# k^T v of six batches moved from the steady stage into the first batch's mixing

## The chip, the cores and the metric

The kernel runs on one core of a Trainium2 chip. The metric is device time in microseconds of one execution. TensorE (PE), VectorE (DVE), ScalarE (ACT) and GpSimd (POOL) compute; SyncE (SP) issues most of the transfers. Each engine works through its own list of instructions in order and waits for the others by semaphores.

## The reference

There are eight batches of 576 tokens, eight heads of 64. All of it is float32.

```python
kv  = einsum('bhsd,bhse->bhde', k, v)          # per head: k^T v, 64 x 64, over 576 tokens
out = einsum('bhsd,bhde->bhse', q, kv)
x   = out / sqrt(mean(out*out, -1) + 1e-6) * g_norm
theta = x @ w_theta                            # 512 x 512
y   = w_tok_r @ (x*cos(theta)) + w_tok_i @ (x*sin(theta))   # over tokens
u   = x + y;  x2 = u + relu(u @ w_ch)
h   = relu(x2^T @ w_tok1) @ w_tok2;  u2 = x2 + h^T
result = u2 + relu(u2 @ w_ch1) @ w_ch2         # 512 -> 1536 -> 512
```

## The kernel before

Most products are made of three float16 matmuls (a value is split into a high and a low half; high by high, high by low, low by high). Only k^T v (line 304), q times k^T v (line 324) and the transposes of batch 0 are float32 matmuls.

A batch goes through units, which are generators: each call of `go` first moves all pending units on by one step and then starts a new one. The units are `kv` (K, two parts per batch), `attend` (a or n, one per row tile r0 to r4), `rotate` (r: theta, sine and cosine, the operands zh and zl), `mix` (M, eight units of 27 matmuls: two column chunks by four output tiles), `channel` (C), `token1` (H) and `token2` (T). Strings and dictionaries in the loop over batches (lines 822 to 870) say which units of the next batches stand beside which unit of the current one. The order of instructions on each engine follows from there: a list scheduler takes the program's order as priority, lets ready instructions of lower priority run ahead, and gives out the eight PSUM banks (line 51) and the buffers of the tile pools as they come free. `urgent` and `placed` raise some instructions or tie them to others.

The row tiles of k and v have 128, 128, 128, 96 and 96 tokens (`ROWS`). `load_kv` (line 266) brings one row tile of k and of v by two transfers from SyncE. Batch 0's last two pairs have buffers in the pool `kp`; everything else goes through three buffers per tensor in the pool `fp`. `load_heads` issues the first three pairs of a batch and its q; the last two pairs are issued by `kv`, after the step that follows the part that frees a buffer. `kv` (line 295) multiplies a row tile of k with one of v for each head and sums over the row tiles in one PSUM bank; after the second part, ScalarE copies half the heads and VectorE the other half into the one operand `kvbd`, which is block-diagonal (two heads in 128 x 128) and was set to zero once on GpSimd (line 123). `attend` multiplies q by it.

Before the loop over batches stand batch 0's k^T v, attention and rotation, the decoding and splitting of the mixing weights, and batch 1's k^T v. The mixing units of batch 0 stand beside the attention of batch 1 and the decoding of w_ch. Batch 2's k^T v stands among the token units of batch 0, which run while batch 1 mixes; that of each later batch stands beside the channel and token units (K00 and K10 in `STEADY`, line 823). The pools `kp` and `stg` end after batch 0's mixing (line 837), and the pools for the later weights take their place. The last rotated tile of batch 0 (`rotate_last`) goes through a transposing transfer from zt into zh (line 457); the last third of the last operand of every mixing unit comes from it.

After the batches come eight pairs of chunks of the last two layers, which are bound by TensorE alone and not touched by the change.

Of the kernel before, what the change touches and what calls it, by code (L numbers as in the profile page):

```python
# [11 lines left out]
F32 = mybir.dt.float32  # L12
I32 = mybir.dt.int32
AF = mybir.ActivationFunctionType
# [5 lines left out]
P = 128  # L20
# [8 lines left out]
def attn_mixer_kernel(  # L29
# [4 lines left out]
    nc = tc.nc  # L34
    B, S, DM = k.shape
    D = g_norm.shape[0]
    H = DM // D
    KD = DM // P
    NR = S // P
# [7 lines left out]
    HP = H // 2  # L47
# [7 lines left out]
    const = const_ctx.enter_context(tc.tile_pool(name="const", bufs=1, side="left"))  # L55
    zp = mix_ctx.enter_context(tc.tile_pool(name="zp", bufs=2, side="left"))
    mp = mix_ctx.enter_context(tc.tile_pool(name="mp", bufs=1, side="left"))
    fp = front_ctx.enter_context(tc.tile_pool(name="fp", bufs=1, side="right"))
    kp = start_ctx.enter_context(tc.tile_pool(name="kp", bufs=2, side="right"))
# [59 lines left out]
    nc.gpsimd.memset(eps, 1e-6)  # L119
    hpi = const.tile([P, 1], F32, name="hpi")  # L120
    nc.gpsimd.memset(hpi, HALF_PI)
    kvbd = const.tile([P, HP, P], F32, name="kvbd")
    nc.gpsimd.memset(kvbd, 0.0)

    def pair(shape, name, pool=const):
        return pool.tile(shape, F16, name=name + "h", bufs=1), pool.tile(shape, F16, name=name + "l", bufs=1)
# [137 lines left out]
    KV = ((0, 1), (2, 3, 4))  # L264

    def load_kv(o, r):
        b, n = o.b, ROWS[r + 1] - ROWS[r]

        pool, bufs = (kp, 2) if b == 0 and r > 2 else (fp, 3)
        for t, src in (("k", k), ("v", v)):  # L270
            dst = pool.tile([P, DM], F32, tag=t, name=f"{t}{b}{r}", bufs=bufs)[:n]
            nc.sync.dma_start(dst, src[b, ROWS[r]:ROWS[r + 1], :])
            o.kv.append(dst)

    def load_heads(b):
        o = Batch()
        o.b, o.zh = b, None
        o.kv = []
        for r in range(3 if b else NR + 1):
            load_kv(o, r)  # L280
        o.q = fp.tile([P, HP, SM + P], F32, tag="q", name=f"q{b}", bufs=1)
        qs = qT[b].rearrange("h p s -> p h s")
        if b == 0:
            nc.sync.dma_start(o.q[:, :, :P], qs[:, :, :P])
        else:
            load_q(o, 0)
        return o
# [7 lines left out]
    def kv(o, part):  # L295

        if part == 0:
            o.kp = bank(f"kvp{o.b}")[:, :HP * D].rearrange("p (h e) -> p h e", h=HP)
        for r in KV[part]:
            kt, vt = o.kv[2 * r:2 * r + 2]  # L300
            for hp in range(HP):
                for i in range(2):
                    cs = slice((2 * hp + i) * D, (2 * hp + i + 1) * D)
                    nc.tensor.matmul(
                        o.kp[i * D:(i + 1) * D, hp, :], kt[:, cs], vt[:, cs],
                        start=r == 0 and hp == 0, stop=r == NR and hp == HP - 1,
                    )
        if part:
            nc.scalar.activation(kvbd[:D, :, :D], o.kp[:D], AF.Copy)
            nc.vector.tensor_copy(kvbd[D:, :, D:], o.kp[D:])  # L310
        yield
        for r in KV[part]:
            if len(o.kv) < 2 * (NR + 1):
                load_kv(o, r + 3)

    def attend(o, r):

        b = o.b
        if r == 0:
            o.R = mp.tile([P, KD, S], F32, tag="R", name=f"R{b}", bufs=2)  # L320
            o.x, o.xt = {}, {}
        po = bank(f"po{b}{r}")
        for hp in range(HP):
            nc.tensor.matmul(po[:, hp * P:(hp + 1) * P], o.q[:, hp, r * P:(r + 1) * P], kvbd[:, hp, :], start=True, stop=True)  # L324
        po3 = po.rearrange("p (h d) -> p h d", d=D)
        ss = fp.tile([P, H], F32, tag="ss", name=f"ss{b}{r}", bufs=3)
        ri = fp.tile([P, H], F32, tag="ri", name=f"ri{b}{r}", bufs=3)
        xs = fp.tile([P, 2, DM], F16, tag="xs", name=f"xs{b}{r}", bufs=2) if b else None
        x = o.x[r] = fp.tile([P, DM], F32, tag="x", name=f"x{b}{r}", bufs=NR + 1)
        xt = o.xt[r] = fp.tile([P, 2, KD, P], F16, tag="xt", name=f"xt{b}{r}", bufs=NR + 1)  # L330

        x3 = x.rearrange("p (h d) -> p h d", d=D)
        place = beside(o)
        yield
        place(nc.scalar.activation(x3, po3, AF.Square, scale=D**-0.5))
        yield
        place(nc.vector.tensor_reduce(ss, x3, axis=AX.X, op=ALU.add))
        nc.gpsimd.tensor_tensor(ss, ss, eps, ALU.add)
        nc.gpsimd.tensor_tensor(ri, ss, mhalf, ALU.pow)  # L339
        yield  # L340
        yield
        place(nc.vector.tensor_tensor(x3, po3, ri.unsqueeze(2).to_broadcast([P, H, D]), ALU.mult))
        n = SR if r == NR else P
        R, by = o.R[:, :, r * P:r * P + n], SW if r == NR else gs
        if b == 0:

            yield
            px = bank(f"px{r}").rearrange("p (k t) -> p k t", k=KD)
            for kk in range(KD):
                nc.tensor.transpose(px[:, kk, :], x[:, kk * P:(kk + 1) * P], ident)  # L350
            yield
            split(xt[:, 0], xt[:, 1], px, 1.0)
            nc.scalar.activation(R, px[:, :, :n], AF.Copy, scale=by)
            return
        if b > 1:
            yield
        place(nc.scalar.activation(xs[:, 0, :], x, AF.Copy))
        yield
        place(nc.vector.tensor_tensor(xs[:, 1, :], x, xs[:, 0, :], ALU.subtract))
        place(nc.sync.dma_start_transpose(xt.rearrange("p a k t -> p (a k) t"), xs.rearrange("p a d -> p (a d)")))  # L360
        for _ in range(3 if b > 1 else 2):
            yield
        place(nc.scalar.activation(R, xt[:, 0, :, :n], AF.Copy, scale=by))
        yield
        place(nc.vector.scalar_tensor_tensor(R, xt[:, 1, :, :n], by, R, ALU.mult, ALU.add))
# [374 lines left out]
    def go(unit, lead=False):  # L740
        advance()
        next(unit)
        (leading if lead else pending).append(unit)
# [16 lines left out]
    def spare(n=1):  # L760
        for _ in range(min(n, len(extra))):
            go(extra.pop(0))

    def front(unit, o, r):
        if o is not None:
            go(unit(o, r))

    tk, cp, first = [], [], iter(())
    for j in range(KD):
        if j == KD - 1:  # L770
            o = load_heads(0)
# [15 lines left out]
    nxt = load_heads(1)  # L787
# [6 lines left out]
    MIX, CHANNEL, TOKEN2 = ([f"{k}{c}{i}" for c in range(2) for i in range(KD)] for k in "MCT")  # L794
    TOKEN1 = [f"H{c}{i}" for c in range(2) for i in range(KJ)]
    UNITS = {"M": mix, "C": channel, "H": token1, "T": token2}

    def run(units, o, nxt, after, also):

        for u in units:  # L800
            kind, c, i = u[0], int(u[1]), int(u[2])
            if kind == "K":
                front(kv, after, c)
            else:
                go(UNITS[kind](o, c, i), True)
            for what in also.get(u, "").split():
                if what == "w":
                    spare()
                elif what == "l":
                    if o.b + 2 < B:  # L810
                        loaded.append(load_heads(o.b + 2))
                elif what[0] == "a":
                    front(attend, nxt, int(what[1]))
                elif what[0] == "n":
                    front(attend, after, int(what[1]))
                elif what[0] == "r":
                    front(rotate, nxt, int(what[1]))
                elif what == "f":
                    next(first, None)

    loaded = []
    TOKENS1 = ["K00", "H00", "H01", "K10", "H10", "H11"]
    STEADY = MIX[:6] + CHANNEL[:2] + MIX[6:] + CHANNEL[2:4] + ["K00"] + CHANNEL[4:] + TOKENS1[1:] + TOKEN2
    BESIDE = {
        "M00": "a2", "M01": "a3", "M02": "a4 l w", "M03": "r0", "M11": "r1", "M12": "r2",
        "C03": "r4", "C10": "w", "H01": "r3 w", "H11": "n0", "T01": "n1 w", "T12": "w",
# [1 line left out]
    for b in range(B):  # L828
        loaded.clear()
        if b == 0:  # L830
            run(MIX, o, nxt, None, {
                "M00": "a0 w", "M01": "a1 w", "M02": "a2 w", "M03": "a3 w", "M10": "a4 r0 w", "M11": "r1 l w", "M12": "r2 w", "M13": "w",
            })
            after = loaded[0]
            spare(len(extra))
# [5 lines left out]
            src, _ = words(w_tok1)  # L841
# [10 lines left out]
            before = o  # L852
        elif b == 1:
            run(MIX[:4], o, nxt, None, {})
            run(["K00"] + TOKEN1 + ["K10"] + TOKEN2, before, None, nxt, {"T00": "n0", "T02": "n1", "T10": "n2 w", "T12": "n3"})
            run(MIX[4:6] + CHANNEL[:1], o, nxt, None, {"M10": "a4 l"})
            after = loaded[0]
            run(STEADY[STEADY.index("C01"):], o, nxt, after, {
                "C01": "r0", "M12": "r1", "M13": "r2", "C03": "r4", "C10": "w", "H01": "r3 w", "H11": "n0", "T01": "n1 w", "T12": "w",
            })  # L860
        elif b + 2 < B:
            at = STEADY.index("M02") + 1
            run(STEADY[:at], o, nxt, None, BESIDE)
            after = loaded[0]
            run(STEADY[at:], o, nxt, after, BESIDE)
        elif b + 2 == B:
# [6 lines left out]
            before, after = o, None  # L873
# [17 lines left out]
        o, nxt = nxt, after  # L891
# [52 lines left out]
```

## Time and profile before

| | |
|---|---|
| three runs | 1104.88, 1108.42, 1108.13 us (median 1108.13) |
| the profiled execution | 1103.0 us, span 1101.2 us |
| mean granted TensorE clock | 0.994 |
| busy: PE, DVE, ACT, POOL | 1066.4, 812.7, 565.7, 186.7 us |
| transfers | 126.31 MB, mean 115 GB/s |

Times in the profile are counted from the start of the span. A busy TensorE counts overlapping matmuls once; a matmul's own duration is longer than the distance from its start to the next start. The granted clock is a mean over a stretch, as a share of full speed. In the timeline, the bracket behind a row is the idle time ahead of it and what ended it.

### The profile page before, as it was taken

The page shows a single profiled execution, that of the slowest core. Times are in us where ns is not written, and L with a number is a line of the kernel's source. Part 1 is how long each engine was busy: PE and PEld are TensorE (multiplying, and loading weights), DVE is VectorE, ACT ScalarE, POOL GpSimd, SP SyncE. Part 2 cuts the span into 40 slices and gives each one's busy share as a digit, 9 for nine tenths or more (in the row PEclk, how much of TensorE's full clock was granted, in tenths as well). Part 3 has the DMA queues.
Part 4 walks back from the last instruction along what each step waited for, and adds up shares of the span by engine and source line. Part 5 has one row for each costly group of instructions (what it writes and reads, how often), then busy time and mean ns, then how long its engine had stood idle before and what let it go on. Part 6 is the DMA issues. An engine that isn't in the chain of part 4 may idle for free.

```text
span 1101.2 us, 21603 instructions
## 1 busy us (share of the span) xinstructions
PE 1066.4 (97%) x8884; PEld 813.7 (74%) x8884; DVE 812.7 (74%) x1475; ACT 565.7 (51%) x966; POOL 186.7 (17%) x252
## 2 busy tenths in 40 slices
PE   4779999999999999999999999999999999999998
PEld 4466776767777678776877777777777777777776
DVE  4989868887988869877654685758586775758484
ACT  3857536556465654646431645446363645446360
POOL 2250032442814518243001000000000000000000
PEclk9989999999999999999999999999999999999999
DMA  9725675867748668472456402020201102020101
GB/s 311 263 69 144 139 193 130 227 156 186 230 107 222 172 165 242 96 175 69 102 205 202 162 23 65 11 76 2 85 3 39 50 22 66 12 76 1 44 1 44
DMA packets 146626, 126.31 MB, mean 115 GB/s; under 512 B 93216, under 2 KB 123040, under 8 KB 146528
## 3 DMA queue, kind: packets, MB, share of 16 engines
q1 hardware_dynamic: 141152, 104.49, 35.1%
q0 software_dynamic: 5376, 20.45, 5.1%
q8 instruction: 69, 1.13, 0.4%
q14 instruction: 29, 0.24, 0.1%
HBM read 74.25 MB, written 29.88 MB: 95 GB/s over the span
## 4 chain that ended last, share of the span: by engine, by line
PE 86%; DVE 7%; DMA 3%; ACT 1%; issue 1%; SPq 1%; POOL 0%; ACTq 0%; DVEq 0%
PE py L104 5%; PE py L105 5%; PE py L103 5%; PE na L103 4%; PE na L105 4%; PE pa L105 4%; PE pa L104 4%; PE pa L103 4%; PE na L104 4%; PE po L324 3%; PE pr L103 2%; PE pr L104 2%; PE pr L105 2%; PE pt L104 2%; PE nc L105 2%; PE nc L103 2%
## 5 line engine op out<-in xcount | busy, mean ns | idle before, releaser
L103 PE MATMUL py<-wmh,zh 128*128 128x256 f16 (+1 forms) x576 | 165.5, 288 | 3.9 <-DMA zh<-zt 2.4
L104 PE MATMUL py<-wml,zh 128*128 128x256 f16 (+1 forms) x576 | 165.4, 288 | 0.0
L105 PE MATMUL py<-wmh,zl 128*128 128x320 f16 (+1 forms) x512 | 146.4, 287 | 0.0
L105 PE MATMUL na<-gh,wbl 128*128 128x288 f16 x384 | 109.3, 286 | 0.0
L104 PE MATMUL pa<-o,wah 128*128 128x288 f16 x384 | 109.2, 286 | 0.0
L104 PE MATMUL na<-gl,wbh 128*128 128x288 f16 x384 | 109.1, 286 | 0.0
L103 PE MATMUL pa<-o,wah 128*128 128x288 f16 x384 | 108.4, 286 | 0.0
L105 PE MATMUL pa<-o,wal 128*128 128x288 f16 x384 | 107.8, 286 | 0.0
L103 PE MATMUL na<-gh,wbh 128*128 128x288 f16 x384 | 106.0, 286 | 0.2
L625 DVE TENSOR_TENSOR gl<-sum,gh 128x1152 f16<-128x1152 f32 x48 | 65.0, 1354 | 21.9 <-ACT gh L624 21.9
L104 PEld LDWEIGHTS <-wbh 128*128 128x128 f16 x672 | 65.7, 98 | 17.7 <-issue 1.0
L104 PEld LDWEIGHTS <-wah 128*128 128x128 f16 x672 | 65.8, 98 | 16.6
L103 PEld LDWEIGHTS <-wah 128*128 128x128 f16 x672 | 65.8, 98 | 16.6
L103 PEld LDWEIGHTS <-wbh 128*128 128x128 f16 x672 | 65.7, 98 | 16.6
L105 PEld LDWEIGHTS <-wal 128*128 128x128 f16 x672 | 65.8, 98 | 16.6
L105 PEld LDWEIGHTS <-wbl 128*128 128x128 f16 x672 | 65.7, 98 | 16.6
L105 PE MATMUL pr<-uh,wcl 128*128 128x256 f16 (+1 forms) x256 | 73.1, 286 | 0.0
L104 PE MATMUL pr<-ul,wch 128*128 128x256 f16 (+1 forms) x256 | 73.1, 286 | 0.0
L103 PE MATMUL pr<-uh,wch 128*128 128x256 f16 (+1 forms) x256 | 73.0, 286 | 0.0
L103 PEld LDWEIGHTS <-zh 128*128 128x128 f16 x576 | 56.7, 98 | 19.8 <-DMA zh<-zt 2.6
L339 POOL TENSOR_TENSOR ri<-ss,mhalf 128x8 f32<-128x8 f32 x40 | 68.8, 1720 | 2.5
L624 ACT ACTIVATE gh<-sum 128x1152 f16<-128x1152 f32 x48 | 55.5, 1156 | 25.6 <-DVE sum L672 25.6
(297 smaller groups left out, 2855.1 us busy)
## 6 DMA issues: line engine op xcount, KB each, us to landing
c<-u2d SPq DMA_DIRECT2D x32, 288.0 KB, 4.3
out<-c SPq DMA_DIRECT2D x64, 144.0 KB, 1.8
q<-in_q SPq DMA_DIRECT2D x7, 1152.0 KB, 6.5
k<-in_k SPq DMA_DIRECT2D x24, 256.0 KB, 5.6
v<-in_v SPq DMA_DIRECT2D x24, 256.0 KB, 5.7
wa_r<-in_w_ch SPq DMA_DIRECT2D x24, 256.0 KB, 4.1
wb_r<-in_w_ch SPq DMA_DIRECT2D x24, 256.0 KB, 4.4
wad<-wa POOLq DMA_DIRECT2D x24, 224.0 KB, 4.0
```

What stands on the lines that cost most here:

```text
L103: nc.tensor.matmul(acc, ah, bh, start=first and i == 0, stop=False, **more)
L104: nc.tensor.matmul(acc, ah, bl, start=False, stop=False, **more)
L105: nc.tensor.matmul(acc, al, bh, start=False, stop=last and i == n - 1, **more)
L324: nc.tensor.matmul(po[:, hp * P:(hp + 1) * P], o.q[:, hp, r * P:(r + 1) * P], kvbd[:, hp, :], start=True, stop=True)
L339: nc.gpsimd.tensor_tensor(ri, ss, mhalf, ALU.pow)
L624: nc.scalar.activation(h.hi[:, 3:], h.s, AF.Copy)
L625: nc.vector.tensor_tensor(h.lo[:, 3:], h.s, h.hi[:, 3:], ALU.subtract)
```

## The change

`kvbd` becomes a list of eight operands, one per batch, each set to zero at the start: those of batches 0 and 1 in `kp`, the others in `fp`, where the buffers of k and v were. k and v of all batches go through a ring of five buffers per tensor in `kp`. Batches 0 and 1 load all five pairs in `load_heads`. Each part of `kv` of batch 1 to 6 then issues the loads of the same row tiles of the next batch, which take the buffers that its matmuls free. The twelve parts of batches 2 to 7 stand in a list, `products`, and a new mark "k" in the dictionary of batch 0's mixing starts the next of them: two beside each of M00 to M03, M10 and M11. The units K00 and K10 leave the token units and `STEADY`. In `kv` the loads stand ahead of the yield.

```diff
-    kvbd = const.tile([P, HP, P], F32, name="kvbd")
-    nc.gpsimd.memset(kvbd, 0.0)
+    kvbd = [(fp if b > 1 else kp).tile([P, HP, P], F32, name=f"kvbd{b}", bufs=1) for b in range(B)]
+    for t in kvbd:
+        nc.gpsimd.memset(t, 0.0)
...
     def load_kv(o, r):
         b, n = o.b, ROWS[r + 1] - ROWS[r]
-
-        pool, bufs = (kp, 2) if b == 0 and r > 2 else (fp, 3)
         for t, src in (("k", k), ("v", v)):
-            dst = pool.tile([P, DM], F32, tag=t, name=f"{t}{b}{r}", bufs=bufs)[:n]
+            dst = kp.tile([P, DM], F32, tag=t, name=f"{t}{b}{r}", bufs=NR + 1)[:n]
...
+    batches = [Batch() for _ in range(B)]
+    for b, o in enumerate(batches):
+        o.b, o.zh, o.kv = b, None, []
+
     def load_heads(b):
-        o = Batch()
-        o.b, o.zh = b, None
-        o.kv = []
-        for r in range(3 if b else NR + 1):
-            load_kv(o, r)
+        o = batches[b]
+        if b < 2:
+            for r in range(NR + 1):
+                load_kv(o, r)
...
         if part:
-            nc.scalar.activation(kvbd[:D, :, :D], o.kp[:D], AF.Copy)
-            nc.vector.tensor_copy(kvbd[D:, :, D:], o.kp[D:])
-        yield
-        for r in KV[part]:
-            if len(o.kv) < 2 * (NR + 1):
-                load_kv(o, r + 3)
+            nc.scalar.activation(kvbd[o.b][:D, :, :D], o.kp[:D], AF.Copy)
+            nc.vector.tensor_copy(kvbd[o.b][D:, :, D:], o.kp[D:])
+        if 0 < o.b < B - 1:
+            for r in KV[part]:
+                load_kv(batches[o.b + 1], r)
+        yield
...
-            if kind == "K":
-                front(kv, after, c)
-            else:
-                go(UNITS[kind](o, c, i), True)
+            go(UNITS[kind](o, c, i), True)
...
+                elif what == "k":
+                    go(kv(*products.pop(0)))
...
-    TOKENS1 = ["K00", "H00", "H01", "K10", "H10", "H11"]
-    STEADY = MIX[:6] + CHANNEL[:2] + MIX[6:] + CHANNEL[2:4] + ["K00"] + CHANNEL[4:] + TOKENS1[1:] + TOKEN2
+    products = [(batches[b], part) for b in range(2, B) for part in range(2)]
+    STEADY = MIX[:6] + CHANNEL[:2] + MIX[6:] + CHANNEL[2:] + TOKEN1 + TOKEN2
...
-                "M00": "a0 w", "M01": "a1 w", "M02": "a2 w", "M03": "a3 w", "M10": "a4 r0 w", "M11": "r1 l w", "M12": "r2 w", "M13": "w",
+                "M00": "a0 k k w", "M01": "a1 k k w", "M02": "a2 k k w", "M03": "a3 k k w", "M10": "a4 k k r0 w",
+                "M11": "r1 l k k w", "M12": "r2 w", "M13": "w",
...
-            run(["K00"] + TOKEN1 + ["K10"] + TOKEN2, before, None, nxt, {"T00": "n0", "T02": "n1", "T10": "n2 w", "T12": "n3"})
+            run(TOKEN1 + TOKEN2, before, None, nxt, {"T00": "n0", "T02": "n1", "T10": "n2 w", "T12": "n3"})
```

## Rows read from the trace of the kernel before

**Rows 1.** The page: TensorE's share of the span, and its granted clock in 40 slices.

```profile
PE 1066.4 (97%) x8884; PEld 813.7 (74%) x8884; DVE 812.7 (74%) x1475; ACT 565.7 (51%) x966; POOL 186.7 (17%) x252
...
PE   4779999999999999999999999999999999999998
...
PEclk9989999999999999999999999999999999999999
```

**Rows 2.** Waits of TensorE, whole span: for whom, us in total, times, longest.

```profile
PE kvp L304 <- DMA v<-in_v: 14.9, 5, 10.4
...
PE py L103 <- DMA zh<-zt: 2.4, 1, 2.4
PE po L324 <- DVE x L342: 1.9, 1, 1.9
```

**Rows 3.** Stretches: busy time of each engine, granted clock, DMA share and GB/s.

```profile
18.00:36.00 18.00, 12.69 (x77) 10.00 (x73) 14.56 (x25) 10.98 (x19) 8.20 (x8) 1.00 1.04 393
47.00:57.00 10.00, 6.92 (x138) 5.79 (x133) 9.94 (x15) 7.53 (x13) 0.00 (x0) 0.81 0.77 249
57.00:67.00 10.00, 6.88 (x47) 5.75 (x46) 10.00 (x16) 9.44 (x16) 5.29 (x4) 0.84 0.26 96
67.00:77.00 10.00, 9.74 (x72) 8.41 (x73) 9.28 (x16) 4.08 (x9) 7.68 (x5) 0.83 0.00 0
77.00:87.00 10.00, 7.62 (x51) 5.48 (x50) 4.80 (x9) 3.41 (x8) 1.04 (x1) 0.85 0.59 119
87.00:97.00 10.00, 10.00 (x60) 5.83 (x59) 10.00 (x21) 6.78 (x14) 2.06 (x2) 0.98 0.88 250
140.00:480.00 340.00, 337.93 (x2963) 246.25 (x2962) 276.90 (x500) 189.22 (x342) 136.74 (x190) 1.00 0.69 179
```

**Rows 4.** Instructions on the tile kvp: count, duration ns (min/median/max), first and last start.

```profile
L304 PE MATMUL kvp<-v,k x640: 220/222/369, 10.4 to 476.5; 128*64 128x64 f32 x96, 96*64 96x64 f32 x64
...
L310 DVE COPY kvbd<-kvp x8: 427/428/428, 19.1 to 477.6; 64x256 f32<-64x256 f32 x8
```

**Rows 5.** Timeline of TensorE, 183 to 198 us: start, duration, what.

```profile
183.48 1.15 PE L304 MATMUL kvp<-v,k 128*64 128x64 f32 x32
184.56 0.31 PE L103 MATMUL pr<-uh,wch 128*128 128x320 f16 x1
...
196.37 1.62 PE L304 MATMUL kvp<-v,k 128*64 128x64 f32 x48
198.01 0.39 PE L535 MATMUL ph<-xt,w1h 128*128 128x512 f16 x1
```

**Rows 6.** Timeline of TensorE, 83 to 99 us: mixing units.

```profile
83.64 0.27 PE L105 MATMUL py<-wmh,zh 128*128 128x256 f16 x1
...
85.94 0.47 PE L105 MATMUL py<-wmh,zh 128*128 128x320 f16 x1
...
95.94 0.30 PE L105 MATMUL py<-wmh,zl 128*128 128x320 f16 x1
...
99.20 0.30 PE L105 MATMUL py<-wmh,zh 128*128 128x320 f16 x1
```

**Rows 7.** Timeline of VectorE at 79 us.

```profile
79.29 0.68 DVE L452 TENSOR_TENSOR zt<-cs,zt 128x512 f16<-128x512 f32 x1
```

**Rows 8.** Timeline of TensorE, 51 to 54 us: batch 1's product.

```profile
51.83 0.69 PE L304 MATMUL kvp<-v,k 96*64 96x64 f32 x16 [1.44 <-DMA v<-in_v]
53.19 1.06 PE L304 MATMUL kvp<-v,k 96*64 96x64 f32 x16 [0.68 <-DMA v<-in_v]
```

**Rows 9.** Timeline of GpSimd, 1 to 24 us.

```profile
1.33 0.52 POOL L123 MEMSET kvbd<- 128x512 f32 x1
...
23.16 0.58 POOL L338 TENSOR_TENSOR ss<-ss,eps 128x8 f32<-128x8 f32 x1 [18.81 <-DVE ss L337]
```

**Rows 10.** Timeline of SyncE's queue, 54 to 82 us.

```profile
54.66 0.44 SPq L272 DMA_DIRECT2D v<-in_v  x1
80.00 1.37 SPq L457 DMA_TRANSPOSE zh<-zt  x1
```

More of the change, by code (lines that the diff above doesn't have):

```diff
@@ L323, in attend @@
         for hp in range(HP):
-            nc.tensor.matmul(po[:, hp * P:(hp + 1) * P], o.q[:, hp, r * P:(r + 1) * P], kvbd[:, hp, :], start=True, stop=True)
+            nc.tensor.matmul(po[:, hp * P:(hp + 1) * P], o.q[:, hp, r * P:(r + 1) * P], kvbd[b][:, hp, :], start=True, stop=True)
         po3 = po.rearrange("p (h d) -> p h d", d=D)
```

## The prediction

> **What bounds the kernel now.** I read the page first. TensorE is busy 97% of the span, and in the 40 slices it is at 9 from the fourth on; its granted clock dips only at the start [rows 1]. So from about 90 us every microsecond of TensorE work is a microsecond of time, and nothing is lost ahead of it except near the start. The waits of TensorE name what is lost: 14.9 us for v (10.4 of it the first load, which the change leaves), then one late transpose of zt, one late x, one late zh [rows 2]. The stretches show where [rows 3] (the columns are the length, the busy time of PE, PEld, DVE, ACT and POOL, the granted clock, the DMA share and GB/s). Between 47 and 87 us TensorE is busy 6.92 + 6.88 + 9.74 + 7.62 = 31.2 of 40 us, so 8.8 us are idle, and its clock is 0.81 to 0.85 of full, which by two levels (1.2 and 2.4 GHz) means 0.19 + 0.16 + 0.17 + 0.15 of each ten us at half, doubled: 13.4 us at the lower level. Of these some 12 are busy, and half of that, 6 us, is work that the full clock would have done besides. In the same stretch VectorE is full (9.94 and 10.00 of 10) until about 77: it decodes and splits the mixing weights and rotates batch 0, and the last tile of batch 0 is what the mixing units wait for. From 140 to 480 TensorE is busy 337.9 of 340 at full clock. So there are 8.8 + 6 = 14.8 us of free room for TensorE between 47 and 87, and next to none after it.
>
> **The change, part by part.**
>
> *The products leave the steady stage.* One batch's k^T v is 80 matmul records (640 for eight batches [rows 4]). In the steady stage a block of 32 takes 183.48 to 184.56 and a block of 48 takes 196.37 to 198.01 until the next matmul starts [rows 5]: 1.08 + 1.64 = 2.72 us. Six batches: 16.3 us less there, on the path, since TensorE is full. Their twelve evacuations (0.43 us on VectorE each [rows 4]) leave too, from engines that have slack there (VectorE 276.9 of 340).
>
> *The same 16.3 us enter batch 0's mixing.* The work is conserved, so the gain is what part of the 14.8 us of room it fills, less what it delays. Four terms:
>
> (a) How much can be done before the mixing units get their last operand, at about 83.4 us. k and v of a batch are 2 x 576 x 512 x 4 bytes = 2.36 MB. At the 393 GB/s that the transfers reached between 18 and 36 [rows 3] that is 6.0 us, at the 249 GB/s of 47 to 57 it is 9.5. The ring holds one batch, so batch 2 starts to load as batch 1's rows are consumed, at about 47, and can be done at 55 to 58; by 83.4 five batches fit at the upper rate, three at the lower. The transfers stood at 96 and 0 GB/s from 57 to 77, so the engines of the DMA are free; I take four: 4 x 2.72 = 10.9 us.
>
> (b) What they push out. PSUM has eight banks. Before the late operand, five mixing units stand in five banks, each with 24 of its 27 matmuls done; their last ones run 83.64 to 85.94 [rows 6]. A product waiting for its evacuation holds a bank. A unit of 256 columns costs, by M12's 3.26 us between its first and ninth low product [rows 6] scaled by 256/320, 2.6 us. I take one and a half units that no longer run ahead: 3.9 us; bounds 0 and 5.2.
>
> (c) What they do to VectorE. Four copies ahead of the last tile's subtraction at 79.29 [rows 7], behind which the transpose and the mixing units stand: 4 x 0.43 = 1.7 us. An evacuation queued behind a product that lacks its load would also hold ScalarE and VectorE; bound: in batch 1 TensorE waited 1.44 and 0.68 us for v in the middle of a product [rows 8], 2.1 a batch, 8.5 us for four; below, nothing.
>
> (d) After 83.4. The gap of 2.4 us for zt [rows 2] is filled, so the half-clock stretch behind it should go: at 0.85 of full over ten us it covers 3 us [rows 3], worth 1.5. Against it, the last two batches land beside the transposes of batch 1; I charge 1.3 us of waits, near the 1.44 of [rows 8].
>
> *Batch 1 keeps all five row tiles in the ring.* Its last two pairs no longer wait for slots until 47; the 2.1 us of [rows 8] and the slow stretch behind them are part of the room above and counted there. They are 0.79 MB earlier, 2.0 us at 393 GB/s among loads of 20 to 36 us, where the transfer engines are full; what hides it is that the last mixing weights to arrive are not yet being decoded. If that cover is gone it costs those 2 us on VectorE.
>
> *Eight operands instead of one.* Seven more memsets on POOL at 0.52 us, 3.6 us, from 1.33 on; POOL then sits idle for 18.8 us before its next work for attention at 23.16 [rows 9]. Nothing, unless the two scalings by g_norm that stand between them hold the first weight: 3.6 us is then the bound. No evacuation waits any more for the attention of the batch before; no wait of that kind is among the largest of [rows 2], so I count nothing for it.
>
> Sum at 83.4: 10.9 - 3.9 - 1.7 = 5.3; with (d) 5.3 + 1.5 - 1.3 = 5.5 us gained. The profiled execution took 1103.0, so 1097.5 on that scale. The median of the three runs is 1108.1, 5 us over the profiled one, and I put the gain on the median: **1102.6 us**.
>
> **Rivals.**
>
> *A. All the room is filled.* TensorE takes any product that is there whenever the mixing lacks a weight, is never idle and never falls to the lower level. Gain up to 14.8, less two of copies: 13 us, 1095. For it: the transfers are idle just then and TensorE's waits are short and many. Against it: DMA in (a), banks in (b).
>
> *B. It cancels.* VectorE is the bound up to 77, and each product adds a copy and a wait to it and takes a bank from the mixing. With (c) at 1.7 + 4 and (b) at 5.2 the 10.9 are gone: 1108. For it: VectorE at 10.00 of 10. Against: a delayed VectorE leaves TensorE products to do meanwhile. This also covers a planner that puts most products behind the late operand, where they fill nothing: the work has then only changed places.
>
> *C. The load queue stands still (slower).* SyncE issues in order. After 54.66 its next transfer is the transpose of zt, at 80.00 [rows 10]: 25 us in which the queue is stuck behind VectorE. Loads of the ring that are ordered behind it wait that long. Then only batches 2 and 3 are in by 80, and four batches, 9.44 MB, come after. In order, TensorE reaches M12 only after the last product; in the trace that lies 12.5 us behind 83.4 (M12's first low product at 95.94 [rows 6]). The loads take 24.0 us at 393 GB/s, 37.9 at the 250 of 87 to 97 [rows 3]; add 2 for landing and subtract the 12.5 and the 16.3 saved later. Net -2.8 at the upper rate, +11.1 at the lower: 1119. It decides from 26.8 us, that is under 352 GB/s. The Trainium skill ("DMA: Bandwidth & Descriptors", Specifications) gives about 358 GB/s as one core's share of HBM; [rows 3] show 393 over 18 us, so the measurement stands over it, but by the page's figure the loads would take an estimated 26.4 us and this rival would stand almost at its turning point even in a clean stretch. For C: 192 KB and 256 KB loads beside transposes ran at 250. Against: the planner can place ring loads ahead of the transpose, as it placed batch 2's first three pairs ahead of it in this trace.
>
> **How the numbers follow.** About 0.3% (3.3 us) is what this kernel's runs can tell from no change. The forecast (gain 2.5 to 9) has 0.45, of which 0.04 lies under 3.3; A 0.17, B 0.20, C 0.18. Faster 0.41 + 0.17 = 0.58, same 0.04 + 0.20 = 0.24, slower 0.18. Range: down to the full room, 1093, and up to 1113, which takes in C as far as a rate of about 300 GB/s and leaves out its lower half; the forecast's own range is 1099 to 1106.
>
> **What would show it.** In the changed profile: products of six batches between about 47 and 100 and none from 140 on, with the steady stretch shorter by some 16 us; TensorE's idle time between 47 and 87 down from 8.8 to about 3 and its clock near 1; transfers at 250 to 400 GB/s from 57 to 77 where there were none; the subtraction of zt at 80 to 83; three or four mixing units ahead of it instead of five. The prediction is wrong if TensorE's waits for k and v in that stretch sum to more than 8 us (C), if the transpose of zt comes after 88 (B), or if the steady stage doesn't shorten by what six batches cost there.

## The result, and the profile after

The changed kernel takes 1117.3 us (median of four runs, 1115.5 to 1118.3) against 1108.3 for the kernel before (four runs, 1104.9 to 1108.4): ratio 1.0087, 95% interval 1.0064 to 1.0111. It is slower by 9 us; 1102.6 was predicted, with 1113 as the upper end of the range.

The profiled execution took 1118.3 us, its span is 1116.6. The page of the changed kernel: TensorE is busy 4.7 us longer than in [rows 1] although it has the same 8884 matmuls, and the granted clock dips in two more slices and deeper in a third.

```profile
PE 1071.1 (96%) x8884; PEld 814.5 (73%) x8884; DVE 817.2 (73%) x1475; ACT 566.4 (51%) x966; POOL 186.7 (17%) x259
...
PEclk9878999999999999999999999999999999999999
```

The waits of TensorE in the changed kernel, whole span. Beside [rows 2], the wait for v has grown by 2.7 us, and three waits are new or larger: token1 (`ph`) for the transposed tile, mixing for zl, token2 (`pu`) for VectorE.

```profile
PE kvp L306 <- DMA v<-in_v: 17.6, 8, 10.8
PE ph L537 <- DMA xt<-xs: 7.7, 7, 1.6
PE py L105 <- DVE zl L414: 5.3, 3, 2.5
...
PE pu L103 <- DVE R L554: 2.0, 5, 0.4
```

The same stretches as in [rows 3], changed kernel (length; busy time of PE, PEld, DVE, ACT, POOL; granted clock; DMA share; GB/s):

```profile
47.00:57.00 10.00, 6.03 (x136) 4.90 (x136) 9.94 (x15) 7.92 (x13) 0.00 (x0) 0.82 0.78 232
57.00:67.00 10.00, 8.07 (x124) 7.05 (x123) 8.71 (x13) 8.11 (x13) 4.74 (x2) 0.83 0.61 177
67.00:77.00 10.00, 7.52 (x84) 5.68 (x86) 7.90 (x13) 3.75 (x9) 2.32 (x3) 0.66 0.64 176
77.00:87.00 10.00, 6.58 (x91) 5.53 (x87) 6.78 (x14) 4.39 (x10) 0.03 (x1) 1.00 0.79 207
87.00:97.00 10.00, 8.56 (x83) 6.67 (x83) 3.81 (x7) 2.51 (x5) 1.81 (x2) 0.66 1.11 280
140.00:480.00 340.00, 334.51 (x2638) 244.49 (x2637) 286.00 (x525) 190.46 (x350) 133.45 (x186) 1.00 0.56 143
```

Between 47 and 97 us TensorE now idles 13.2 us (8.8 before), and the clock takes 10.3 us of work away (6.9 before; one minus the clock, times ten, for each stretch, so idle time is counted with it). More work stands in the stretch and less room is used. VectorE, full before, has 3.81 of 10 at the end of it.

Where in the program the time went can be read from one instruction, the first channel matmul of batch 0, which ends the mixing stage. First the kernel before (the last attention of batch 1, its first rotation, that first channel matmul), then the changed one:

```profile
79.99 1.05 PE L324 MATMUL po<-kvbd,q 128*128 128x128 f32 x8
...
86.21 0.63 PE L103 MATMUL pt<-wth,xt 128*128 128x512 f16 x1
...
105.59 0.27 PE L103 MATMUL pr<-uh,wch 128*128 128x256 f16 x1
```

```profile
88.44 0.80 PE L306 MATMUL kvp<-v,k 128*64 128x64 f32 x10 [3.01 <-DMA v<-in_v]
...
103.71 1.05 PE L326 MATMUL po<-kvbd,q 128*128 128x128 f32 x8
...
105.92 0.39 PE L103 MATMUL pt<-wth,xt 128*128 128x512 f16 x1
...
130.17 0.27 PE L103 MATMUL pr<-uh,wch 128*128 128x256 f16 x1
...
217.23 0.39 PE L537 MATMUL ph<-xt,w1h 128*128 128x512 f16 x1 [1.31 <-DMA xt<-xs]
```

Up to that matmul both kernels run the same matmuls but for the 480 of the moved products. The stage ends 24.6 us later, for 16.3 us of products: nothing was filled and 8.3 us were lost (4.4 of idle time and 3.4 of clock from the stretches above, 0.5 of idle time behind 97). From there to the end of the span it is 986.4 us against 995.6: only 9.2 less, not 16.3. The other 7 are the new waits at token1 and token2 (7.7 + 2.0, against 2.0 of waits in the same part before). 8.3 + 7.1 is the 15.4 us by which the spans differ.

The medians differ by 9 only, because the first profile of before (1103.0) was 5 us shorter than the median and that of the changed kernel was the longest of its four runs; e9 below is a second profile of before.

### The profile page after: what moved, and what is told of

Its sections match the earlier page's. It is cut to its first block, busy times and chain, and to the rows that moved or that the text cites. A ratio compares the mean times of both kernels' runs of the same rounds, so it can differ in the third digit from the quotient of the medians.

```text
span 1116.6 us, 21631 instructions
## 1 busy us (share of the span) xinstructions
PE 1071.1 (96%) x8884; PEld 814.5 (73%) x8884; DVE 817.2 (73%) x1475; ACT 566.4 (51%) x966; POOL 186.7 (17%) x259
## 4 chain that ended last, share of the span: by engine, by line
PE 65%; DVE 14%; DMA 10%; ACT 6%; issue 2%; POOL 1%; SPq 1%; ACTq 0%; DVEq 0%; POOLq 0%
PE na L103 4%; PE pa L103 4%; PE pa L105 4%; PE pa L104 4%; PE na L105 4%; PE na L104 4%; PE py L103 3%; DMA xt<-xs 3%; PE py L105 3%; PE py L104 3%; PE pc L105 2%; PE pc L104 2%; PE pc L103 2%; PE nc L105 2%; PE nc L103 2%
## 5 line engine op out<-in xcount | busy, mean ns | idle before, releaser
L103 PE MATMUL py<-wmh,zh 128*128 128x320 f16 (+1 forms) x576 | 166.0, 288 | 2.3 <-DMA zh<-zt 1.4
L104 PE MATMUL py<-wml,zh 128*128 128x320 f16 (+1 forms) x576 | 166.0, 288 | 0.0
```

Source lines behind the costliest of these rows:

```text
L103: nc.tensor.matmul(acc, ah, bh, start=first and i == 0, stop=False, **more)
L104: nc.tensor.matmul(acc, ah, bl, start=False, stop=False, **more)
```

## The experiments

Medians are compared with runs of the kernel before on the same chip, between 1107.1 and 1108.1.

**e1: the kernel before without a product between the token units.**

```diff
-    TOKENS1 = ["K00", "H00", "H01", "K10", "H10", "H11"]
-    STEADY = MIX[:6] + CHANNEL[:2] + MIX[6:] + CHANNEL[2:4] + ["K00"] + CHANNEL[4:] + TOKENS1[1:] + TOKEN2
+    TOKENS1 = ["K00", "H00", "H01", "H10", "H11"]
+    STEADY = MIX[:6] + CHANNEL[:2] + MIX[6:] + CHANNEL[2:4] + ["K00", "K10"] + CHANNEL[4:] + TOKENS1[1:] + TOKEN2
```

> The kernel before with one edit: both parts of each later batch's k^T v stand ahead of the last four channel units, so none stands between the token units of the first and of the second chunk. Same work, same place otherwise. Theory 1 (the product covered the landing of the last transposed tile): TensorE waits 1 to 1.6 us ahead of the second chunk's token units in each of five or six batches, 5 to 8 us in all, so 1113 to 1116 against about 1108. Rival (the waits of the changed kernel come from another place, e.g. later transposes): no change, 1108, and no such waits.

1122.0 us, ratio 1.0121 (1.0091 to 1.0150), above the 1113 to 1116 that theory 1 gave. The waits at token1 came, in three turns instead of five or six, and the 2.0 us at token2 exactly as in the changed kernel; but with both parts together the waits for v grow as well (20.8 against 14.9 us), so the run doesn't weigh the cover alone. TensorE's waits in e1:

```profile
PE kvp L304 <- DMA v<-in_v: 20.8, 14, 10.7
...
PE ph L535 <- DMA xt<-xs: 4.7, 3, 2.1
...
PE pu L103 <- DVE R L552: 2.0, 5, 0.4
```

**e2: other work in the place of the cover.** The same edit stands in batch 1's dictionary.

```diff
-        "C03": "r4", "C10": "w", "H01": "r3 w", "H11": "n0", "T01": "n1 w", "T12": "w",
+        "C03": "r4", "C10": "w", "H01": "r3 n0 n1 w", "T01": "w", "T12": "w",
```

> The changed kernel with one edit: the attention of the next batch's tiles 0 and 1 both stand beside unit H01 instead of H11 and T01, which puts another 1.05 us of TensorE work between the token units of the two chunks. Theory 1: most of the 5.5 us of waits for the transposed tile and of the 2.0 us at token2 go, 1111 to 1113 against 1117. Rival: no change.

1113.3 us, ratio 1.0048 (1.0033 to 1.0063): 4.0 us under the changed kernel, 0.3 above the 1111 to 1113 expected. The token2 wait is gone; the token1 wait falls only from 7.7 to 5.4, which is not most of it (e2's waits):

```profile
PE ph L537 <- DMA xt<-xs: 5.4, 8, 1.2
```

**e3: no loads for the moved products.**

```diff
-            kt, vt = o.kv[2 * r:2 * r + 2]
+            kt, vt = (batches[1] if o.b > 1 else o).kv[2 * r:2 * r + 2]
...
-        if 0 < o.b < B - 1:
-            for r in KV[part]:
-                load_kv(batches[o.b + 1], r)
```

> The changed kernel, with the loads of k and v of batches 2 to 7 left out (their products read batch 1's tiles, so these products are not the reference's). Theory 2 (in batch 0's mixing TensorE, in order, stands at products whose loads come late, behind the transpose of zt in SyncE's queue and short of bandwidth): the mixing stage loses 8 us or more, 1103 to 1109. Rival 3 (the products hold PSUM banks, so that fewer mixing units run ahead of the last operand; loads don't matter): only 1 to 4 us less, 1113 to 1116, and the idle time between 47 and 97 us stays near 13 us.

1117.2 us, ratio 1.0081 (1.0054 to 1.0108): the total doesn't move, so late loads alone are not the cause, and theory 2 as I put it is wrong. But the mixing stage does end 10.6 us earlier, and later waits for ScalarE, VectorE and the second zt give it back: 7.3 us between 130 and 165, none of which the changed kernel has, and 1.7 more by a granted clock of 0.83 from 140 to 150. TensorE's timeline in e3:

```profile
119.59 0.27 PE L103 MATMUL pr<-uh,wch 128*128 128x256 f16 x1
...
130.68 0.30 PE L103 MATMUL pr<-uh,wch 128*128 128x320 f16 x1 [0.48 <-ACT uh L483]
...
132.32 0.30 PE L104 MATMUL pr<-ul,wch 128*128 128x320 f16 x1 [1.34 <-DVE ul L486]
...
140.16 0.28 PE L103 MATMUL py<-wmh,zh 128*128 128x256 f16 x1 [1.54 <-ACT zh L408]
...
141.60 0.28 PE L105 MATMUL py<-wmh,zl 128*128 128x256 f16 x1 [1.05 <-DVE zl L411]
...
151.17 0.28 PE L103 MATMUL py<-wmh,zh 128*128 128x256 f16 x1 [1.61 <-DMA zh<-zt]
...
163.14 0.28 PE L103 MATMUL pu<-w2h,hh 128*128 128x256 f16 x1 [1.28 <-ACT hh L71]
```

**e4: the copies of the moved products cut to one column per head.**

```diff
-            nc.scalar.activation(kvbd[o.b][:D, :, :D], o.kp[:D], AF.Copy)
-            nc.vector.tensor_copy(kvbd[o.b][D:, :, D:], o.kp[D:])
+            e = D if o.b < 2 else 1
+            nc.scalar.activation(kvbd[o.b][:D, :, :e], o.kp[:D, :, :e], AF.Copy)
+            nc.vector.tensor_copy(kvbd[o.b][D:, :, D:D + e], o.kp[D:, :, :e])
```

> The changed kernel, with the evacuations of batches 2 to 7 cut to one column of 64 per head on both engines (the rest of these operands stays zero, so the attention of these batches is not the reference's). If the copies on VectorE and ScalarE delay the rotation of batch 0 (step c of the prediction): 2 to 5 us less than 1117. If loads or banks are the cause: within 1 us of 1117.

1117.4 us (ratio 1.0080, 1.0051 to 1.0109): nothing. With the loads and the order as they are, the copies cost no time.

**e5: batch 1's attention ahead of the products** (on e2).

```diff
-"M00": "a0 k k w", "M01": "a1 k k w", "M02": "a2 k k w", "M03": "a3 k k w", "M10": "a4 k k r0 w",
+"M00": "a0 a1 a2 k k w", "M01": "a3 a4 k k w", "M02": "k k w", "M03": "k k w", "M10": "k k r0 w",
```

> The kernel of e2 with one edit: batch 1's five attention units stand beside the first two mixing units of batch 0, ahead of all products but the first two parts. Theory 4 (in the changed kernel the products, two behind each attention, push batch 1's attention from 56-81 us to 57-104, VectorE is idle 12 of the 30 us from 77 to 107, and its work is missing later): VectorE busy over 23 of these 30 us, 1105 to 1109. Theory 2 (late loads alone): the waits for v stay, 1111 to 1115. If the late last operand counts (attention ahead of batch 0's rotation on VectorE): zt after 85 us and no gain.

1115.4 us, ratio 1.0076 (1.0059 to 1.0093): theory 4 alone is wrong too. The attention is early, but TensorE now waits for v instead, 8.5 us between 20 and 140 us, and VectorE still has only 18.4 of the 30 us from 77 to 107. Two lines of e5, its waits in that window and its stretch from 77 to 107:

```profile
PE kvp L306 <- DMA v<-in_v: 8.5, 9, 2.2
```

```profile
77.00:107.00 30.00, 21.78 (x279) 17.10 (x277) 18.38 (x35) 11.03 (x23) 0.89 (x1) 0.88 1.11 291
```

**e6: all products behind the last operand** (on e2; the lines of the dictionary after the edit).

```diff
+"M00": "a0 w", "M01": "a1 w", "M02": "a2 w", "M03": "a3 w", "M10": "a4 r0 w",
+"M11": "r1 l k k k k w", "M12": "r2 k k k k w", "M13": "k k k k w",
```

> The kernel of e2 with one edit: all twelve product parts stand behind the last three mixing units of batch 0 (four beside each of M11, M12, M13), where TensorE has no idle time. Theory 4: the stretch up to 88 us is as in the kernel before, the products add their 16.3 us there and save them later, 1107 to 1110. Theory 2: only one batch fits the ring, so five batches load one after the other while TensorE has little else: at 6.0 to 9.5 us a batch 30 to 47 us of loads beside 36 us of work, 1113 to 1120 with waits for v of 6 us or more.

1123.9 us, ratio 1.0146 (1.0124 to 1.0168), 10.5 us of waits for v between 20 and 140. Here TensorE does stand at late loads, as theory 2 said.

**e7: products spread thinner** (on e2; the lines after the edit).

```diff
+"M00": "a0 w", "M01": "a1 k w", "M02": "a2 k w", "M03": "a3 k k w", "M10": "a4 k k r0 w",
+"M11": "r1 l k k w", "M12": "r2 k k w", "M13": "k k w",
```

> The kernel of e2 with one edit: the twelve parts are spread thinner and start later (one beside M01 and M02, two beside M03, M10, M11, M12 and M13). The attention of batch 1 stays nearer to its old order, and loads have longer to land. Theories 2 and 4 both expect less than e2's 1113.3: 1107 to 1111. If banks decide (a product in flight costs a mixing unit wherever it stands): 1112 to 1115.

1110.5 us, ratio 1.0029 (1.0019 to 1.0040): inside what was expected, 2.8 under e2, still above before.

**e8: only two batches moved**, on the kernel before, ring of three as it was.

```diff
+    EARLY = 3
+    kvbd = [(fp if b > 1 else kp).tile([P, HP, P], F32, name=f"kvbd{b}", bufs=1) for b in range(EARLY + 1)]
+    kvbd += [kvbd[2 + b % (EARLY - 1)] for b in range(EARLY + 1, B)]
...
+        if part and 0 < o.b < EARLY:
+            for r in range(3):
+                load_kv(batches[o.b + 1], r)
...
-                front(kv, after, c)
+                if after is not None and after.b > EARLY:
+                    go(kv(after, c))
...
+    products = [(batches[b], part) for b in range(2, EARLY + 1) for part in range(2)]
...
-                "M00": "a0 w", "M01": "a1 w", "M02": "a2 w", "M03": "a3 w", "M10": "a4 r0 w", "M11": "r1 l w", "M12": "r2 w", "M13": "w",
+                "M00": "a0 k k w", "M01": "a1 k k w", "M02": "a2 w", "M03": "a3 w", "M10": "a4 r0 w", "M11": "r1 l w", "M12": "r2 w", "M13": "w",
...
```

> The kernel before with one part of the change: only batches 2 and 3 have their products beside M00 and M01 of batch 0 (two parts each), through the old ring of three buffers, with two operands more; batches 4 to 7 stay at K00 and K10. The room in 47 to 70 us could take their 5.4 us: if the room is real, 1103 to 1106. If a product displaces attention and mixing units as soon as it is there (theory 4), 1107 to 1111.

1103.2 us, ratio 0.9965 (0.9952 to 0.9978): faster. The mixing stage of e8 ends where it did in the first profile of before, with two batches' products inside it:

```profile
105.90 0.27 PE L103 MATMUL pr<-uh,wch 128*128 128x256 f16 x1
```

So the room is real for most of 5.4 us of products; not to a microsecond, since the same stage ends at 103.1 in the second profile of before (e9) and at 108.5 in e11. The turn that lost its product (batch 1's) has a new token1 wait of 0.98 us.

**e9: the kernel before, profiled again.** No edit.

> The kernel before, profiled once more: the first profile (1103.0) lies 4 to 5 us under the median of its runs. Expected 1105 to 1109, and the place where the two profiles differ. If it is again 1103, profiling itself is kinder to this kernel.

1108.1 us, span 1106.2. The mixing stage ends at 103.1, 2.5 us *earlier* than in the first profile, and the execution is 5 us longer: TensorE waits for zh, zl and the second zt from 120 to 128, for v, hh and hl from 143 to 147, and runs at 0.94 of its clock from 140 to 200. These stretches of e9 answer to the first profile's, which had 43.00 of 43 and 58.64 of 60 busy:

```profile
97.00:140.00 43.00, 40.22 (x359) 29.20 (x357) 36.41 (x82) 26.75 (x56) 0.00 (x0) 1.00 0.49 99
140.00:200.00 60.00, 56.97 (x478) 40.74 (x476) 42.69 (x85) 30.44 (x57) 15.12 (x18) 0.94 0.61 152
```

**e10: e5 without loads** (the edits of e5 and of e3).

> The kernel of e5 (attention first, with the cover of e2), with the loads of k and v of batches 2 to 7 left out (their products read batch 1's tiles, so these products are not the reference's). In e3 the mixing stage ended 10.6 us earlier without loads and later waits for VectorE and ScalarE gave it back; in e5 the attention was early but the loads were waited for. If both limits hold together: the stage ends at 117 to 121 us as in e3, the waits from 130 to 165 us go, and the total is 1100 to 1106. If VectorE is late for another reason: 1110 or more, with the same waits as e3.

1106.3 us, ratio 0.9995 (0.9983 to 1.0007), 0.3 above the 1100 to 1106 expected of the two limits together. Without loads, e3 gained nothing; with the attention ahead, dropping the loads gains 9.1 us (from e5). The stage ends at 113.8 (expected 117 to 121). The waits behind it did not go, as I had expected, but fell from 7.3 to 5.3: 1.33 for zh, 1.05 for zl, 2.89 for zt. So the two limits hold together, and a third remains. Two things are not separated here: e5 and e10 have the cover of e2 and e3 has not, and without the loads both the queue of SyncE and the traffic beside the transposes are gone.

**e11: e8 with the cover** in batch 1's turn, the edit of e2 there alone.

> The kernel of e8 with one edit: in batch 1's turn, where no product stands between the token units of the two chunks any more, the attention of tiles 0 and 1 of the next batch stands there. Theory 1: one wait of 1 us and one of 0.4 go, 1102 against e8's 1103.2. Rival: moving the attention forward costs as much, 1103 to 1104.

1102.1 us, ratio 0.9950 (0.9935 to 0.9965). The median is 1.1 under e8's and the intervals overlap; against the kernel before it is faster by half a per cent, the best version here that has all the products.

**e12: no products and no loads of the six batches at all.**

```diff
-        if 0 < o.b < B - 1:
-            for r in KV[part]:
-                load_kv(batches[o.b + 1], r)
...
-                    go(kv(*products.pop(0)))
+                    pass
```

> The changed kernel with the products and loads of batches 2 to 7 left out altogether (their operands stay zero, so the output of these batches is not the reference's). It shows what taking the products out of the steady stage is worth with nothing put elsewhere. Theory 1 (their cover is missing): 16.3 less the 7 us of new waits, 1097 to 1100 against 1107.5. If the waits come from the mixing stage's delay instead: 1090 to 1093.

1096.2 us, ratio 0.9893 (0.9878 to 0.9909): 12 us, a little better than the 1097 to 1100 of theory 1 and far from the rival's 1090 to 1093. The waits at token1 and token2 are all there although nothing was added anywhere (e12):

```profile
PE ph L534 <- DMA xt<-xs: 7.8, 7, 1.5
...
PE pu L103 <- DVE R L551: 2.0, 5, 0.4
```

From e12 to the changed kernel it is 21.1 us: the price of 16.3 us of products and of their loads in the mixing stage. In the prediction's terms, 16.3 us were to be saved and 10.8 paid; 12.0 were saved and 21.1 paid.

## Why the prediction was wrong

**"Six batches: 16.3 us less there, on the path."** The duration was right; the products' place was not free. In the steady order a product stood between the token units of the two chunks, and the transposed tile of the last channel units landed behind it. Without it TensorE waits there ([rows 5] show the product and token1 right behind it at 198.01; the changed kernel's row at 217.23 shows the wait). I asked what hides each added edit and never what the removed one hid; this term stood at nothing. It is 7 us of the 16.3 in the profile, and 4.3 by the medians of e12, where the waits appear with nothing else added and 12.0 of the 16.3 are gained. In e2 other work in that place gives 4.0 back.

**Step (a), four batches by 83.4.** By 83.4 TensorE had done 160 of the 480 moved records: two batches. Rival C had the mechanism: the first pair of batch 4 is issued at 66.57 and 68.01, then the queue stands at the transpose of zt, and the next pair goes out at 80.65. The queue of the changed kernel:

```profile
68.01 0.33 SPq L271 DMA_DIRECT2D v<-in_v  x1
77.82 1.36 SPq L459 DMA_TRANSPOSE zh<-zt  x1
79.28 1.27 SPq L362 DMA_TRANSPOSE xt<-xs  x1
80.65 0.53 SPq L271 DMA_DIRECT2D k<-in_k  x1
```

The rest of the four batches then loads beside the transposes, and the last pair goes out at 120 us. Not only the issue is late: once it goes on, the transfer engines are full at a lower rate than in [rows 3]. Their share is 1.11 at 280 GB/s from 87 to 97, and behind that (changed kernel):

```profile
97.00:107.00 10.00, 9.46 (x137) 7.05 (x137) 7.31 (x14) 4.66 (x10) 1.95 (x2) 1.00 1.10 297
107.00:120.00 13.00, 13.00 (x143) 8.38 (x142) 10.13 (x17) 7.53 (x14) 2.34 (x2) 1.00 1.08 354
```

[rows 3] had 393 GB/s at a share of 1.04, with no transpose among its transfers. The Trainium skill ("DMA: Bandwidth & Descriptors", Specifications) gives about 358 GB/s as the HBM limit of one core; these stretches stay under it, while the 393 of [rows 3] stood over it. The 250 GB/s by which I priced C's lower rate was not a rate of such loads: the transfers issued there were weights of 512 KB, q in 1152 and 128 KB, and transposes.

With C's own sum at its lower rate, 1119, the measured time agrees to 2 us, but that is partly luck. TensorE's waits for v between 47 and 97 sum to 4.4 us, under the 8 that were to be C's sign, and e3 has no loads and the same total.

**Step (b), one and a half mixing units pushed out.** Two were (68 mixing matmuls, of three units, stand ahead of the operand instead of 120), near the estimate. What I left out is that the products also pushed out batch 1's *attention*. Two parts stand behind each attention unit, and the planner gave them TensorE's time first: the last attention moved from 80.0 to 103.7 and the first rotation from 86.2 to 105.9. VectorE, which I took as full anyway, then stood idle 12 of 30 us (17.9 busy from 77 to 107, 24.5 before), and batch 1's last rotated tile, the next late operand, goes out at 149.29 instead of 122.97. First the two lines of the kernel before, then those of the changed one:

```profile
77.00:107.00 30.00, 27.62 (x179) 18.04 (x178) 24.53 (x44) 18.71 (x36) 3.10 (x3) 0.94 0.57 141
...
122.97 1.24 SPq L457 DMA_TRANSPOSE zh<-zt  x1
```

```profile
77.00:107.00 30.00, 24.61 (x310) 19.24 (x307) 17.91 (x34) 11.57 (x24) 3.78 (x4) 0.89 1.00 261
...
149.29 1.31 SPq L459 DMA_TRANSPOSE zh<-zt  x1
```

That second operand is a milestone that orders the runs. Of the five kernels with six moved batches and the cover of e2, its issue and the median are: e10 139.3 and 1106.3; e7 146.6 and 1110.5; e2 148.6 and 1113.3; e5 151.8 and 1115.4; e6 162.8 and 1123.9. The end of the mixing stage puts these five in the same order (113.8, 127.6, 129.6, 133.0, 137.3); it is e3 that tells the two apart: without loads the stage ended 10.6 us earlier, the second operand only 1.5 (147.8), and the total stayed. Loads and attention order each limit it, and only e10, which eases both, moves it far. Its issue in e3, then in e10:

```profile
147.79 1.30 SPq L456 DMA_TRANSPOSE zh<-zt  x1
```

```profile
139.26 1.31 SPq L456 DMA_TRANSPOSE zh<-zt  x1
```

That this operand is what costs the time is argued from this order and from e3; no run moves it alone. How much of the rest is due to PSUM banks was not tried.

**Step (c), VectorE delayed by copies.** Wrong in sign and size: the subtraction of zt comes at 77.11, 2.2 us earlier than in [rows 7], and e4 without the copies takes as long. VectorE in the changed kernel:

```profile
77.11 0.68 DVE L454 TENSOR_TENSOR zt<-cs,zt 128x512 f16<-128x512 f32 x1
```

**Step (d), the clock comes back.** Between 77 and 87 it did (1.00). But there are new gaps, 2.5 us for zl at 69 and 3.0 us for v at 88, and the stretches of both stand at 0.66.

**The room of 14.8 us.** It was read correctly and could hold two batches (e8: 3.9 us gained for 5.4 moved), but not six in any order tried. My reading of e9, which no run tests alone, is that after that stage VectorE and ScalarE pace the kernel once more, until about 147 us, so that TensorE's idle time ahead of it is worth less than it looks. My base profile was one of the executions that hardly show this second limit; in the one at the median, TensorE waits 5.8 us between 120 and 148 and loses 3.6 to the clock up to 200.

**The bound for (a) to (d)** reached only to +11 through C and I gave the cover no bound at all. With its 7 us above 1113 the range would have held the result, though not for the right reasons in (a) and (b).

## What to carry to other kernels

Before moving work off a full engine, look at what lands while it runs: its place may be the cover of a transfer, and the saving is its duration less that. Idle time of the bounding engine ahead of a late operand is worth filling only up to the next late operand, so look for that one before pricing the room, and try a part of the move first: two batches of six gave a third of a per cent, half a per cent with a new cover, and six cost 0.9. A ring as deep as one unit of work, fed from a queue that also carries late transfers, lets the loads start only when the consumer has moved.

## What the runs showed of the hardware

TensorE's granted clock did not follow the idle time of a stretch: in the changed kernel 67 to 77 stands at 0.66 with 2.5 us idle, 77 to 87 at 1.00 with 3.4 us idle. Its matmuls are slow right behind some gaps and not behind others: 0.42 us for a mixing matmul from 69.80 on, behind 2.52 us of idle time, and 0.42 again from 89.68 on, behind the 3.01 us at 88.44; behind the 1.42 us at 81.22 it is 0.27. The two profiles of the one unedited program differ by 5.0 us of span, with the difference between 107 and 200 us; a sum made on one profile should be made on one near the median.
